# Reordering small pieces of work in the queues of a fused mLSTM and Fourier-mixing kernel

## Chip, core and metric

The kernel runs on one core of a Trainium2 chip. The metric is the device time of one execution in microseconds (us), the median of three runs. The profile is of one more execution; its span, 418.1 us from the first to the last instruction, is a little shorter than the time of that run, 419.82 us. TensorE is also called PE here, VectorE DVE, ScalarE ACT and GpSimd POOL, as the profile does.

## What is computed

The first half is an mLSTM cell over 4 batches, 8 heads, 768 steps and 40 features per head. The second half takes its output as 4 x 768 x 320, adds the real part of a two-dimensional Fourier transform, normalizes and applies a two-layer MLP with a residual.

```python
# mLSTM, for every step t
m_new = max(f[t] + m, i[t])
C = exp(f[t] + m - m_new) * C + exp(i[t] - m_new) * outer(v[t], k[t])
n = exp(f[t] + m - m_new) * n + exp(i[t] - m_new) * k[t]
y[t] = sigmoid(o[t]) * (C @ q[t]) / max(abs(n @ q[t]), 1)

# mixing, x is y as (4, 768, 320)
u  = x + real(fft(fft(x, axis=1), axis=2))
un = (u - mean(u)) / sqrt(var(u) + 1e-6)
out = u + relu(un @ w_ch1) @ w_ch2          # 320 -> 1280 -> 320
```

## The kernel before

The 768 steps of a batch are cut into six chunks of 128. Within a chunk the recurrence is two products: one from the state that the chunk before left (`from_state`), one from the chunk's own steps, weighed by an exponential and masked (`scores`, `weigh`, `from_chunk`). The result is copied out of PSUM (`gather`), transposed to have the steps on the partitions (`turn`) and divided by its denominator (`finish`). After that a batch is folded, transformed (`mix_seq`, `mix_feat`), added to x with its statistics (`mix_add`), centered, transposed and sent through the MLP. One batch's mLSTM runs beside the batch before's mixing and MLP.

Every engine works off its own instructions in the order in which the program has them. That order is a plan: `at(slot, phase, fn, ...)` puts a function at a slot, and within a slot at a phase. The phases of a slot are `EVAC` (0), `FILL` (1), `MAIN` (2) and `FILL_PE` (3); fractions are added to place a piece before or behind another. Slots are the steps of the MLP of some batch once it has begun (slot 31 for batch 0).

```python
    def mlstm_from_state(b, c):
        k = chunks[b, c]
        k.ph = ps_h.tile([L, NP, L], FP, name="ph", tag="ph")     # two banks serve ph, pc and late px
        if c > 0:
            ...                                                    # k.C x k.qg into k.ph

    def mlstm_to_state(b, c):
        k = chunks[b, c]
        if c < NT - 1:
            k.pc = ps_h.tile([L, NP, D1], FP, name="pc", tag="ph")
            ...                                                    # k.kn x k.vw into k.pc (+ the decayed state)

    def mlstm_gather(b, c):
        ...                                                        # k.pc -> C_next, k.ph -> k.hT
        if 0 < c < TG:                                             # first step of the chunk before
            nc.scalar.copy(out=hT_bufs[(b * NT + c - 1) % 2][:, :, 0:1], in_=k.ph[:, :, 0:1])
        nc.scalar.activation(out=k.so, in_=k.so, func=AF.Tanh, scale=0.5)

    def mlstm_turn(b, c, early):
        k = chunks[b, c]
        k.px = bank("px", [L, NP, L]) if early else ps_h.tile([L, NP, L], FP, name="px", tag="ph")
        for p in range(NP):
            nc.tensor.transpose(k.px[:, p, :], k.hT[:, p, :], ident)

    def plan_mlstm(b, s0, stride=3):
        for c in range(NT):
            s = s0 + stride * c
            ...
            at(s + 1, FILL, mlstm_mask, b, c)                      # b > 0, GpSimd
            at(s + 2, FILL, mlstm_weigh, b, c)                     # VectorE
            at(s + 3, FILL_PE, mlstm_from_state, b, c)
            at(s + 3, FILL_PE + 3, mlstm_from_chunk, b, c)
            at(s + 3, FILL_PE + 3, mlstm_to_state, b, c)
            at(s + 4, FILL, mlstm_gather, b, c)
            if b == 0:
                t, x = ((8, 11), (11, 14), (13, 14), (14, 15.5), (17, 18), (18, 21))[c]
            else:
                t = s + (8, 8, 7, 7 if b == 1 else 5, 5, 5)[c]
                x = t + 1
            at(t, FILL_PE + ((2.5 if c < 4 else 1) if b == 0 else 1), mlstm_turn, b, c, b == 0 and c < 4)
            at(x, FILL + 0.05, mlstm_finish, b, c)
```

The weights arrive as 64-bit floats and are made into 32-bit ones in ten pieces, each in three steps: `take` (VectorE extracts exponent and fraction from the words that a DMA brought), `convert` (ScalarE, two activations), `join` (VectorE, three operations).

```python
    def mlp_relu(b, gr, f):                                        # frees the bank pm
        nc.scalar.activation(out=hidden(gr, f), in_=mixes[b].pm[f % 2], func=AF.Relu, scale=-1.0)

    when += [((s, 0.7), (s + 1, 0.7), (s + 2, 0.6)) for s in (33, 36, 39, 42, 45)]
    ...
        for (s, phase), fn in zip(w, (p.take, p.convert, p.join)):
            at(s, FILL + phase, fn)
```

The addition to x (`mix_add`) frees the bank `pu` of the feature transform, which is then used for `pm` of the MLP. The reciprocal root of the variance is found by a bit trick on VectorE and three Newton steps of four operations on GpSimd; the MLP's output is scaled by it.

```python
    def mix_rstd(b):
        ...                                                        # VectorE: v = -(var + 1e-6) / 2, first y
        for _ in range(3):
            nc.gpsimd.tensor_tensor(out=t, in0=y, in1=y, op=OP.mult)
            nc.gpsimd.tensor_tensor(out=t, in0=t, in1=v, op=OP.mult)
            nc.gpsimd.tensor_scalar(out=t, in0=t, scalar1=1.5, scalar2=None, op0=OP.add)
            nc.gpsimd.tensor_tensor(out=y, in0=t, in1=y, op=OP.mult)
```

Of the kernel before, what the change touches and what calls it, by code (L numbers as in the profile page):

```python
# [10 lines left out]
FP = mybir.dt.float32  # L11
# [3 lines left out]
AF = mybir.ActivationFunctionType  # L15
OP = mybir.AluOpType
# [3 lines left out]
L = 128  # L20
NT = S // L
NP = H // 2
D1 = D + 1
# [3 lines left out]
NFF = DFF // L  # L27
# [23 lines left out]
def kernel(  # L51
# [14 lines left out]
    nc = tc.nc  # L66
# [13 lines left out]
    ps_h = pool("ps_h", 2, space=PSUM)  # L80
    ps_m = pool("ps_m", 1, space=PSUM)

    turn = iter("3210321032120312031230123012012301023130201320132013201320123021320321")
# [38 lines left out]
    def at(slot, phase, fn, *args):  # L122
        plan.setdefault((slot, phase), []).append((fn, args))
# [7 lines left out]
    EVAC, FILL, MAIN, FILL_PE = range(4)  # L131
# [249 lines left out]
    chunks = {}  # L381
# [91 lines left out]
    def mlstm_from_state(b, c):  # L473

        k = chunks[b, c]
        k.ph = ps_h.tile([L, NP, L], FP, name="ph", tag="ph")
        if c > 0:
            for p in range(NP):
                nc.tensor.matmul(k.ph[:, p, :], k.C[:, p, :], k.qg[:, p, :], start=(p == 0), stop=False,  # L479
                                 skip_group_check=True)  # L480
# [8 lines left out]
    def mlstm_to_state(b, c):  # L489
        k = chunks[b, c]  # L490
        if c < NT - 1:
            add = b == 0 and c > 0
            k.pc = ps_h.tile([L, NP, D1], FP, name="pc", tag="ph")
            for h in range(H):
                r0 = (h % 2) * 64
                nc.tensor.matmul(k.pc[r0:r0 + D, h // 2, :], k.kn[:, h, :], k.vw[:, h, :], start=(h < 2), stop=not add,
                                 skip_group_check=True)
            if add:
                for hip in range(2):
                    r = slice(hip * 64, hip * 64 + D)  # L500
                    nc.tensor.matmul(k.pc[r], ident[:, r], k.Cd, start=False, stop=True, skip_group_check=True)

    def mlstm_gather(b, c):
        k = chunks[b, c]
        k.hT = hT_bufs[(b * NT + c) % 2]
        if c < NT - 1:
            for hip in range(2):
                r, m = slice(hip * 64, hip * 64 + D), slice(hip * 64, hip * 64 + D1)
                Cv = k.C_next[r, :, m]
                if b == 0:  # L510
                    nc.scalar.copy(out=Cv, in_=k.pc[r])
                elif c == 0:
                    nc.vector.tensor_copy(out=Cv, in_=k.pc[r])
                else:
                    nc.vector.tensor_tensor(out=Cv, in0=Cv, in1=k.pc[r], op=OP.add)
        if c in BACKWARDS:
            nc.scalar.copy(out=k.hT[:, :, 1:], in_=backwards(k.ph, L - 1, L - 1))
            if c > TG:
                nc.scalar.copy(out=k.hT[:, :, 0:1], in_=k.ph[:, :, 0:1])
            else:  # L520
                nc.gpsimd.tensor_copy(out=k.hT[:, :, 0:1], in_=h_first)
        else:
            for r in (slice(0, L),) if c > 0 else (slice(hip * 64, hip * 64 + D1) for hip in range(2)):
                nc.scalar.copy(out=k.hT[r], in_=k.ph[r])  # L524
            if c == 0:
                nc.gpsimd.tensor_copy(out=h_first, in_=k.hT[:, :, 0:1])
        if 0 < c < TG:
            nc.scalar.copy(out=hT_bufs[(b * NT + c - 1) % 2][:, :, 0:1], in_=k.ph[:, :, 0:1])
        nc.scalar.activation(out=k.so, in_=k.so, func=AF.Tanh, scale=0.5)

    def mlstm_turn(b, c, early):
        k = chunks[b, c]
# [24 lines left out]
# [3 lines that stand above are left out]
            if b > 0:  # L560
                t = 22 + 2 * c if b == 1 and c < 3 else s - 5
                at(t, FILL, mlstm_load, b, c)
                at(t, FILL, mlstm_load_max, b, c)
                at(t, FILL, mlstm_load_decay, b, c)
                at(s, FILL, mlstm_load_o, b, c)
            if (b, c) > (0, 0):
                at(s, FILL, mlstm_exp, b, c, 0)
                at(s + 1, FILL - 0.5, mlstm_exp, b, c, NP)
                last = (b, c) == (0, NT - 1)
                at(s - 1 if last else s, FILL_PE + (2.05 if last else 2), mlstm_scores, b, c)  # L570
                if b > 0:
                    at(s + 1, FILL, mlstm_mask, b, c)
            at(s, FILL, mlstm_scale_v, b, c)
            at(s if (b, c) == (0, 2) else s + 1, FILL + 0.1, mlstm_scale_q, b, c)
            at(s + 2, FILL, mlstm_decay, b, c)
            end = (b, c) == (0, NT - 1)
            at(s + 1 if end else s + 2, FILL - 0.4 if end else FILL, mlstm_weigh, b, c)
            at(s + 2 if end else s + 3, MAIN - 0.1 if s + 3 in slots_of_halves else FILL_PE, mlstm_from_state, b, c)
            at(s + 2 if end else s + 3, FILL_PE + (2 if end else 3), mlstm_from_chunk, b, c)
            at(s + 3, FILL_PE + 3, mlstm_to_state, b, c)  # L580
            at(s + 3 if end else s + 4, FILL, mlstm_gather, b, c)
            if b == 0:
                t, x = ((8, 11), (11, 14), (13, 14), (14, 15.5), (17, 18), (18, 21))[c]
            else:
                t = s + (8, 8, 7, 7 if b == 1 else 5, 5, 5)[c]
                x = t + 1
            at(t, FILL_PE + ((2.5 if c < 4 else 1) if b == 0 else 1), mlstm_turn, b, c, b == 0 and c < 4)
            at(x, FILL + 0.05, mlstm_finish, b, c)


# [4 lines left out]
    mixes = {}  # L595
# [187 lines left out]
    def mix_rstd(b):  # L783

        k = mixes[b]
        v = st_p.tile([L, NT], FP, name="v", tag="v")
        y = k.rstd = st_p.tile([L, NT], FP, name="rstd", tag="rstd")
        t = st_p.tile([L, NT], FP, name="t", tag="t")
        nc.vector.tensor_scalar(out=v, in0=k.u[:, :, DM + 1], scalar1=1e-6, scalar2=None, op0=OP.add)
        nc.vector.tensor_scalar(out=t.bitcast(U32), in0=v.bitcast(U32), scalar1=1, scalar2=None,  # L790
                                op0=OP.logical_shift_right)
        nc.vector.tensor_scalar(out=y.bitcast(U32), in0=t.bitcast(U32), scalar1=-1.0, scalar2=float(0x5F3759DF),
                                op0=OP.mult, op1=OP.add)
        nc.vector.tensor_scalar(out=v, in0=v, scalar1=-0.5, scalar2=None, op0=OP.mult)
        for _ in range(3):
            nc.gpsimd.tensor_tensor(out=t, in0=y, in1=y, op=OP.mult)
            nc.gpsimd.tensor_tensor(out=t, in0=t, in1=v, op=OP.mult)
            nc.gpsimd.tensor_scalar(out=t, in0=t, scalar1=1.5, scalar2=None, op0=OP.add)
            nc.gpsimd.tensor_tensor(out=y, in0=t, in1=y, op=OP.mult)

    def plan_mix(b, s0, x_done, s_feat, s_add, s_turn):
        for j in range(TG):
# [298 lines left out]

    def plan_batch(b, s_mlstm, s_mix, s_mlp):
        plan_mlstm(b, s_mlstm)
        done = [s_mlstm + 3 * (j + NT // 2) + 7 + (b == 1 and j == 0) for j in range(NT // 2)]
        assert s_mix >= done[-1] and s_mlp >= s_mix + 9
        late = [s_mlp + 2 * c for c in range(TG)]
        if b == 0:
            feat = [s_mix + 1, s_mix + 1, s_mlp + 3]
            turn = [s_mix + 2, s_mix + 3, s_mix + 4]
            add = turn + [s_mlp, s_mlp + 4, s_mlp + 6]  # L1110
            late = [s_mlp + 2, s_mlp + 5, s_mlp + 7]
        else:
            feat = [s_mix + c for c in ((3, 4, 6) if b == 1 else (3, 4, 7))]
            add = [s_mix + c for c in ((4, 4, 5, 6, 7, 7) if b == 1 else (4, 4, 5, 6, 8, 9))]
            turn = [s_mix + c for c in ((5, 6, 6) if b == 1 else (6, 7, 8))]
            late = [s_mix + c for c in ((7, 8, 8) if b == 1 else (9, 10, 10))]
            at(s_mlp, EVAC + 0.5, mlp_sums)
        plan_mix(b, s_mix, done, feat, add, turn + late)
        at(s_mlp + NFF + (2 if b > 0 else 0), FILL + 0.6, mix_rstd, b)
        plan_mlp(b, s_mlp)  # L1120

    s_mlp = 31
# [9 lines left out]

    when = [((2, 0.7), (4, 0.5), (6, 0.6)), ((6, 0.7), (7, 0.5), (8, 0.6)), ((11, 0.7), (13, 0.5), (22, 0.6))]
    when += [((22, 0.7), (23, 0.7), (27, 0.6)), ((27, 0.7), (28, 0.7), (32, 0.6))]
    when += [((s, 0.7), (s + 1, 0.7), (s + 2, 0.6)) for s in (33, 36, 39, 42, 45)]
    pieces = w1_pieces + w2_pieces
    for n, (w, p) in enumerate(zip(when, pieces)):
        if n > 4:
# [125 lines left out]
```

## Time and profile before

| what | value |
|---|---|
| time, median of 3 | 420.55 us (419.62 to 420.63) |
| span in the profile | 418.1 us |
| PE matmul busy | 405.1 us, 2966 instructions |
| PE weight load busy | 304.0 us |
| VectorE busy | 287.8 us |
| ScalarE busy | 188.9 us |
| GpSimd busy | 115.3 us |
| granted TensorE clock | 1.0 |

How to read it: an engine's idle time only costs something if the engine that sets the end waits for it. The view of the waits of one engine lists who ended them, with the sum, the number and the longest. The timeline lists instructions in order of time: start, duration, engine, line of the kernel, operation, output and inputs, and in brackets the idle time of the engine just before and what ended it. An instruction that waits for several semaphores is put down to the one that the profile saw last, so a row has to be held against the ends of the instructions it may depend on. In the first third of the span (up to about 125 us) all engines have much to do: in the stretch from 100 to 110 us PE is busy for 10.00 us, VectorE for 9.63, GpSimd for 5.93 and ScalarE for 5.22.

### The profile page before, as it was taken

The numbers are of one execution on the slowest core, as the hardware profiler recorded it, in microseconds if no ns is written. First come the engines' busy times: TensorE is split into PE (matmuls) and PEld (weight loads), VectorE is DVE, ScalarE is ACT, GpSimd is POOL, SyncE is SP. The second block draws the span as 40 slices with busy tenths as digits, with TensorE's granted clock in tenths as the row PEclk, the third lists the DMA queues.
The fourth block names the chain that finished last, engine by engine and source line by source line (L and its number), as shares of the span: only waits on it lengthen the run. The fifth ranks groups of instructions, "written<-read, shape, count | busy, mean of one in ns | idle before, by whom it ended". The sixth has DMA issues, their size and how long they took to land.

```text
span 418.1 us, 8020 instructions
## 1 busy us (share of the span) xinstructions
PE 405.1 (97%) x2966; PEld 304.0 (73%) x2966; DVE 287.8 (69%) x682; ACT 188.9 (45%) x493; POOL 115.3 (28%) x194
## 2 busy tenths in 40 slices
PE   8999999999999999999999999989999999999997
PEld 6877454676667778767559998967559988555996
DVE  8789894767995638786874569786774686335652
ACT  6986375676661232655455413735442113355000
POOL 5564201459431520333061430333050000010000
PEclk9999999999999999999999999999999999999999
DMA  7889298467774154166200444210000000000010
GB/s 225 284 227 346 85 269 260 148 195 226 241 202 148 57 156 144 60 211 179 69 0 2 153 153 131 105 36 2 0 2 0 33 31 29 4 2 0 16 48 31
DMA packets 20549, 47.14 MB, mean 113 GB/s; under 512 B 2784, under 2 KB 9312, under 8 KB 20384
## 3 DMA queue, kind: packets, MB, share of 16 engines
q1 hardware_dynamic: 20512, 46.65, 36.5%
q8 instruction: 23, 0.38, 0.4%
q14 instruction: 14, 0.11, 0.1%
HBM read 42.52 MB, written 4.11 MB: 112 GB/s over the span
## 4 chain that ended last, share of the span: by engine, by line
PE 75%; DVE 14%; DMA 5%; ACT 2%; issue 2%; POOL 0%; DVEq 0%; ACTq 0%; POOLq 0%; SPq 0%
PE po L1031 18%; PE pm L912 16%; PE po L975 8%; PE pm L917 5%; PE ps L465 4%; PE ph L486 4%; DMA kvt<-in_kv 4%; PE ph L479 3%; PE pu L733 3%; PE pm L850 2%; DVE W L471 2%; PE px L535 2%; DMA qk<-in_qkT 2%; PE pz L702 2%; PE put L776 1%
## 5 line engine op out<-in xcount | busy, mean ns | idle before, releaser
L981 DVE SCALAR_TENSOR_TENSOR x<-po,rstd,x 128x160 f32<-128x160 f32 (+1 forms) x69 | 26.9, 394 | 41.2 <-PE po L1031 35.5
L921 DVE TENSOR_TENSOR h<-h,pm 128x384 f32<-128x384 f32 x60 | 30.6, 549 | 32.5 <-PE pm L917 19.4
L421 ACT ACTIVATE W<-W,colT 128x128 f32<-128x128 f32 x144 | 45.0, 396 | 0.0
L443 POOL TENSOR_SCALAR_AFFINE_SELECT W<-W 128x1024 f32<-128x1024 f32 x18 | 21.9, 1218 | 80.6 <-ACT W L421 56.3
L912 PE MATMUL pm<-uT,w_sb 128*128 128x384 f32 x90 | 37.5, 503 | 0.2 <-DVE uT L900 0.2
L975 PE MATMUL po<-w_sb,h 128*128 128x320 f32 x120 | 34.4, 435 | 0.0
L471 DVE TENSOR_TENSOR W<-ps,W 128x512 f32<-128x512 f32 x48 | 30.7, 680 | 4.5 <-POOL W L443 4.3
L850 PE MATMUL pm<-uT,w_sb 128*128 128x384 f32 x80 | 30.0, 500 | 1.6 <-DMA qk<-in_qkT 0.9
L781 ACT COPY uT<-put 128x384 f32<-128x384 f32 x24 | 11.2, 478 | 39.8 <-PE put L776 39.8
L975 PEld LDWEIGHTS po<-w_sb,h 128*128 128x128 f32 x120 | 22.2, 190 | 9.5 <-issue 0.8
L1031 PE MATMUL po<-T,S 128*128 128x160 f32 x180 | 27.9, 302 | 0.3 <-DVE x L981 0.3
L465 PE MATMUL ps<-qk 40*128 40x128 f32 x384 | 27.4, 282 | 0.0
L465 PEld LDWEIGHTS ps<-qk 40*128 40x128 f32 x384 | 23.7, 187 | 4.7 <-issue 0.7
L1031 PEld LDWEIGHTS po<-T,S 128*128 128x128 f32 x180 | 25.5, 190 | 1.7 <-DVE x L981 0.5
L1031 PE MATMUL po<-w_sb,h 128*128 128x160 f32 x180 | 26.4, 301 | 0.0
L1031 PEld LDWEIGHTS po<-w_sb,h 128*128 128x128 f32 x180 | 25.1, 190 | 1.3 <-DVE x L981 0.3
L431 POOL TENSOR_TENSOR qg<-qk,Gb 128x512 f32<-128x512 f32 x18 | 25.7, 1430 | 0.9 <-DMA Gb<-G_d 0.8
L486 PE MATMUL ph<-W,kvt 128*41 128x128 f32 x384 | 25.8, 277 | 0.0
L524 ACT COPY h<-ph 41x512 f32<-41x512 f32 (+1 forms) x16 | 9.3, 583 | 36.2 <-PE ph L486 36.1
L912 PEld LDWEIGHTS pm<-uT,w_sb 128*128 128x128 f32 x90 | 15.5, 189 | 13.7 <-DVE h L921 6.0
L479 PEld LDWEIGHTS ph<-qg,C 128*128 128x128 f32 x160 | 20.0, 191 | 6.3 <-issue 2.6
L479 PE MATMUL ph<-qg,C 128*128 128x128 f32 x160 | 21.6, 278 | 2.9 <-DVE x L550 1.8
(207 smaller groups left out, 845.6 us busy)
## 6 DMA issues: line engine op xcount, KB each, us to landing
W<-M_d SPq DMA_DIRECT2D x18, 512.0 KB
kvt<-in_kv SPq DMA_DIRECT2D x24, 324.0 KB
qk<-in_qkT SPq DMA_DIRECT2D x48, 160.0 KB
raw<-in_w SPq DMA_DIRECT2D x10, 640.0 KB
Gb<-G_d SPq DMA_DIRECT2D x36, 128.0 KB
so<-in_o SPq DMA_DIRECT2D x24, 160.0 KB
out<-x SPq DMA_DIRECT2D x24, 160.0 KB
ds_sb<-in_dft_s SPq DMA_DIRECT2D x1, 1155.0 KB
```

The lines of the kernel that those rows point to most:

```text
L421: nc.scalar.activation(out=k.W[:, h, :], in_=M, func=AF.Exp, scale=-1.0, bias=colT[:, c, 0, b * H + h:b * H + h + 1])
L431: nc.gpsimd.tensor_tensor(out=k.qg, in0=k.qk[:, 0], in1=k.Gb, op=OP.mult)
L465: nc.tensor.matmul(k.ps[hip][:, p, :], k.qk[r, 1, p, :], k.qk[r, 0, p, :], start=True, stop=True)
L471: nc.vector.tensor_tensor(out=Wv, in0=k.ps[hip], in1=Wv, op=OP.mult)
L479: nc.tensor.matmul(k.ph[:, p, :], k.C[:, p, :], k.qg[:, p, :], start=(p == 0), stop=False, skip_group_check=True)
L486: nc.tensor.matmul(k.ph[hip * 64:hip * 64 + D1, p, :], k.v1[:, 2 * p + hip, :], k.W[:, 2 * p + hip, :], start=(c == 0 and p == 0), stop=Tr ...
L850: nc.tensor.matmul(k.pm[i], w1_sb[:, ch, f0:f0 + L], u[2 * ch], start=(ch == 0 and not ahead), stop=(ch == 1 and ahead), skip_group_check= ...
L912: nc.tensor.matmul(bank, w, u, start=start, stop=True, skip_group_check=True)
L921: nc.vector.tensor_tensor(out=h, in0=h, in1=bank, op=OP.add)
L975: nc.tensor.matmul(k.po, hidden(gr, f)[:, i * L:(i + 1) * L], w2_sb[:, f, :], start=(f == 0), stop=(f == NFF - 1))
L981: nc.vector.scalar_tensor_tensor(out=u, in0=po, scalar=k.rstd[:, c:c + 1], in1=u, op0=OP.mult, op1=OP.add)
L1031: nc.tensor.matmul(po, a[:, f], w[:, f], start=start and f == 0, stop=f == half - 1, skip_group_check=True)
```

## The change

Nothing is computed differently. Six things are moved:

- In batch 0, chunk 4, the tile `pc` is taken from the pool ahead of `ph`, so that the two exchange their banks; and the transposes of chunks 0 and 1 stand a slot later, behind the product from the state of the chunk after.
- The conversion and the join of the sixth weight piece are a slot later, so that the conversion, which waits for a DMA by way of VectorE, doesn't stand ahead of relus.
- In batches 1 to 3 the tanh of the output gate stands behind the centering of the same slot.
- The last of batch 0's six additions is a slot earlier.
- Batch 0's first guess of the reciprocal root is two slots later, and its Newton steps are spread three slots apart.
- In batches 2 and 3 the transposes of the fourth chunk, and so its `finish` and the first `fold`, are two slots (the fold one slot) later.

```diff
     def mlstm_from_state(b, c):
         k = chunks[b, c]
+        if (b, c) == (0, NT - 2):
+            k.pc = ps_h.tile([L, NP, D1], FP, name="pc", tag="ph")
         k.ph = ps_h.tile([L, NP, L], FP, name="ph", tag="ph")
...
-            k.pc = ps_h.tile([L, NP, D1], FP, name="pc", tag="ph")
+            if not hasattr(k, "pc"):
+                k.pc = ps_h.tile([L, NP, D1], FP, name="pc", tag="ph")
...
-        nc.scalar.activation(out=k.so, in_=k.so, func=AF.Tanh, scale=0.5)
+        if b == 0:
+            mlstm_tanh(b, c)
+
+    def mlstm_tanh(b, c):
+        so = chunks[b, c].so
+        nc.scalar.activation(out=so, in_=so, func=AF.Tanh, scale=0.5)
...
+            if b > 0:
+                at(s + 4, FILL + 0.35, mlstm_tanh, b, c)
             if b == 0:
-                t, x = ((8, 11), (11, 14), (13, 14), (14, 15.5), (17, 18), (18, 21))[c]
+                t, x = ((9, 11), (12, 14), (13, 14), (14, 15.5), (17, 18), (18, 21))[c]
             else:
-                t = s + (8, 8, 7, 7 if b == 1 else 5, 5, 5)[c]
+                t = s + (8, 8, 7, 7, 5, 5)[c]
                 x = t + 1
-            at(t, FILL_PE + ((2.5 if c < 4 else 1) if b == 0 else 1), mlstm_turn, b, c, b == 0 and c < 4)
+            at(t, FILL_PE + ((1.95 if c < 2 else 2.5 if c < 4 else 1) if b == 0 else 1), mlstm_turn, ...)
...
-        for _ in range(3):
-            ...                                  # the four GpSimd operations
+        k.newton = v, t
+
+    def mix_rstd_step(b):
+        ...                                      # the same four, once
...
-        done = [s_mlstm + 3 * (j + NT // 2) + 7 + (b == 1 and j == 0) for j in range(NT // 2)]
+        done = [s_mlstm + 3 * (j + NT // 2) + 7 + (b > 0 and j == 0) for j in range(NT // 2)]
...
-            add = turn + [s_mlp, s_mlp + 4, s_mlp + 6]
+            add = turn + [s_mlp, s_mlp + 4, s_mlp + 5]
...
-        at(s_mlp + NFF + (2 if b > 0 else 0), FILL + 0.6, mix_rstd, b)
+        s = s_mlp + NFF + 2
+        at(s, FILL + 0.6, mix_rstd, b)
+        for n in range(3):
+            at(s + 3 * n if b == 0 else s, FILL + 0.65, mix_rstd_step, b)
...
-    when += [((s, 0.7), (s + 1, 0.7), (s + 2, 0.6)) for s in (33, 36, 39, 42, 45)]
+    when += [((33, 0.7), (35, 0.7), (36, 0.6))] + [((s, 0.7), (s + 1, 0.7), (s + 2, 0.6)) for s in (36, 39, 42, 45)]
```

More of the change, by code (lines that the diff above doesn't have):

```diff
@@ L581, in plan_mlstm @@
             at(s + 3 if end else s + 4, FILL, mlstm_gather, b, c)
+            if b > 0:
+                at(s + 4, FILL + 0.35, mlstm_tanh, b, c)
             if b == 0:
-                t, x = ((8, 11), (11, 14), (13, 14), (14, 15.5), (17, 18), (18, 21))[c]
+                t, x = ((9, 11), (12, 14), (13, 14), (14, 15.5), (17, 18), (18, 21))[c]
             else:
-                t = s + (8, 8, 7, 7 if b == 1 else 5, 5, 5)[c]
+                t = s + (8, 8, 7, 7, 5, 5)[c]
                 x = t + 1
-            at(t, FILL_PE + ((2.5 if c < 4 else 1) if b == 0 else 1), mlstm_turn, b, c, b == 0 and c < 4)
+            at(t, FILL_PE + ((1.95 if c < 2 else 2.5 if c < 4 else 1) if b == 0 else 1), mlstm_turn, b, c, b == 0 and c < 4)
             at(x, FILL + 0.05, mlstm_finish, b, c)
@@ L794, in mix_rstd @@
         nc.vector.tensor_scalar(out=v, in0=v, scalar1=-0.5, scalar2=None, op0=OP.mult)
-        for _ in range(3):
[L796 to L799, printed above, removed]
+        k.newton = v, t
+    def mix_rstd_step(b):
+        k = mixes[b]
+        y, (v, t) = k.rstd, k.newton
+        nc.gpsimd.tensor_tensor(out=t, in0=y, in1=y, op=OP.mult)
+        nc.gpsimd.tensor_tensor(out=t, in0=t, in1=v, op=OP.mult)
+        nc.gpsimd.tensor_scalar(out=t, in0=t, scalar1=1.5, scalar2=None, op0=OP.add)
+        nc.gpsimd.tensor_tensor(out=y, in0=t, in1=y, op=OP.mult)
     def plan_mix(b, s0, x_done, s_feat, s_add, s_turn):
```

## The prediction

> **What bounds the kernel now.** I read the page's busy line first, then the waits of TensorE, then the timelines of all engines around each wait.
>
> ```profile
> PE 405.1 (97%) x2966; PEld 304.0 (73%) x2966; DVE 287.8 (69%) x682; ACT 188.9 (45%) x493; POOL 115.3 (28%) x194
> ```
>
> TensorE (PE) is busy 405.1 of 418.1 us. The change adds or removes no matmul, so it can only win back idle time: 418.1 - 405.1 = 13.0 us. Of that, 1.25 us lie before the first matmul and about 3 us after the last one (413.51 + 1.52 = 415.0): some 8.7 us are left. The waits of PE say where (total, times, longest, in us):
>
> ```profile
> PE ph L479 <- DVE x L550: 1.8, 3, 1.3
> ...
> PE put L776 <- ACT uc L769: 1.2, 4, 0.4
> PE pm L850 <- DMA qk<-in_qkT: 0.9, 1, 0.9
> PE ph L479 <- POOL eo L622: 0.8, 1, 0.8
> PE px L535 <- ACT h L519: 0.8, 1, 0.8
> PE px L535 <- ACT h L528: 0.8, 2, 0.4
> PE pm L850 <- DVE x L753: 0.5, 1, 0.5
> ```
>
> These seven rows sum to 6.8 us, and the parts of the change aim at most of them. So 420.55 - 8.7 = 411.9 us is the floor if every gap closed, just at the 2% mark (412.1).
>
> The second stage to read is that of slots 33 to 37, in the timeline of all engines from 66 to 78 us (start, duration, engine, line; in brackets the idle time before):
>
> ```profile
> 68.64 0.49 DVE L344 TENSOR_SCALAR e<-raw 128x640 uint32<-128x640 uint32 x1 [6.17 <-DMA raw<-in_w]
> ...
> 69.17 0.83 ACT L351 ACTIVATE e<-e,ebias 128x640 uint32<-128x640 uint32 x1 [3.94 <-DVE e L344]
> ...
> 69.91 0.72 ACT L352 ACTIVATE m<-m 128x640 f32<-128x640 uint32 x1
> 70.53 0.85 ACT L865 ACTIVATE h<-pm 128x384 f32<-128x384 f32 x2
> ...
> 71.05 0.91 PE L850 MATMUL pm<-uT,w_sb 128*128 128x384 f32 x2 [0.90 <-DMA qk<-in_qkT]
> ```
>
> A weight piece lands at 68.6, VectorE (DVE) takes it, ScalarE (ACT) converts it, and only then comes the relu that empties the bank for the next pm matmul. That relu's input was complete at about 66.2 (last L841). The matmul starts at 71.05, right after the first relu's end (70.53 + 0.48 = 71.0): the wait is the relu's, not the DMA's that the row names.
>
> The third is batch 3's fifth chunk:
>
> ```profile
> 278.32 0.49 DVE L550 TENSOR_TENSOR x<-px,so 128x320 f32<-128x320 f32 x1
> 278.96 1.13 PE L479 MATMUL ph<-qg,C 128*128 128x128 f32 x8 [1.26 <-DVE x L550]
> ```
>
> PE's ph needs the bank from which VectorE has just finished the third chunk; the two px groups before it (275.37 and 277.10) took both banks of that pool.
>
> **What the Trainium skill says.** "PSUM — Partial Sum Buffer", section "Engine vs sequencer instructions": the queues of ScalarE, VectorE and GpSimd are strict FIFO, and matmuls start and complete in program order. The trace agrees: the relu sat behind a conversion that was itself waiting, with ScalarE idle for 3.94 us. "Perfetto Trace Analysis", section "Tensor Engine Instruction": the profiler estimates a matmul's end, so I reckon from starts: four transposes are listed at 0.66 us, but the next group starts 0.49 us after them (23.44 to 23.93). "SBUF — State Buffer", section "SBUF: two separate sides": GpSimd and a VectorE operation with two SBUF inputs take turns on one port pair for whole instructions. The trace fits: Newton's first operations on 128x6 take 0.78, 0.66 and 0.81 us beside VectorE, later ones 0.20.
>
> **The change part by part.**
>
> *First batch (0 to 54 us).* Transposes of chunks 0 and 1 now stand behind the next chunk's ph. At 23.44 and 29.06 px waited 0.41 and 0.40 for the last small copy (L528 ends at 23.38); ph needs only the state copies (22.71). So ph starts at about 22.93 (end of the pM group), px follows at 23.8 with its input ready. Gain up to the second transpose: 0.41 + 0.40 = 0.8, with restart about 0.9. It doesn't all survive. VectorE runs without a real gap from 24.5 to 41 us and does not move, so px of chunk 3 must wait for chunk 1's finish (bank read until 34.60 + 0.49 = 35.09); it started at 35.78, so 0.65 is left. The rest of the chain then shifts with it: state copies, ph of chunk 5 (39.74 to about 39.05), its output, copy, last px (43.12 to 42.4). VectorE's weighing of chunk 5 ends at 39.95, still ahead of its use (40.55). The pc/ph exchange of chunk 4 swaps two banks: ph of chunk 5 starts at 39.74 while ph of chunk 4 is still being copied (39.66 to 40.25), so it already stands in pc's bank; I give the swap nothing. **0.7 us.**
>
> *Conversion and addition (66 to 78 us).* The conversion moves one slot later, behind the relus: the 0.90 gap goes (0.97 by starts). The scores behind it then wait until VectorE has weighed both ps banks (70.73), some 0.4 us of that back. Then put waits 0.28 for uc, which sat behind so's tanh (0.37 by starts) and ScalarE's late queue; the earlier relu and the tanh behind it free it. Then pm waits 0.52 for the addition L753 that frees the bank of pu (76.77 to 77.26); the addition now stands a slot earlier, ahead of the join (2.4 us) and the next piece's extraction (0.9 us), at about 72 to 73 us. Starts: 0.97 + 0.35 + 0.59 = 1.9, and the scores' 0.4 falls inside time that put then no longer waits. **1.85 us.**
>
> *Newton's steps (92 to 118 us).* Twelve GpSimd operations stood between 91.92 and 97.27, ahead of the mask:
>
> ```profile
> 97.35 1.09 POOL L443 TENSOR_SCALAR_AFFINE_SELECT W<-W 128x1024 f32<-128x1024 f32 x1
> 98.41 1.28 POOL L431 TENSOR_TENSOR qg<-qk,Gb 128x512 f32<-128x512 f32 x1
> ```
>
> The mask's other inputs are there by about 94.3 (the copies of h), so mask, weighing and qg come 3 us earlier, and VectorE, full from 98.5 to 118, starts its backlog earlier. PE waited 0.30 (99.74, for qg) and 0.17 (117.26, for a finish). Three steps of four operations, three slots apart, cost about 0.9 us each and fit: rstd is first used ten slots after the first. **0.45 us.**
>
> *Fourth chunks' transposes of batches 2 and 3 (two slots later).* ph of chunk 5 then finds a bank that was free long ago. The waits of 0.38 (184.34) and 1.26 (278.96) go; by starts 0.55 and 1.43. Against it: finish (1.7 us) and fold (1.7 us) of this chunk now stand in VectorE's queue behind the weighing and ahead of the next finish and the addition L921. In batch 3: state copy until 284.0, weighing to 285.3, finish 287.0, fold 288.7, next finish 290.4, L921 290.95, which the tails L917 want at about 290.85 (292.25 now, less 1.43). So 0.15 to 0.2 us may come back in each. **0.35 + 1.25 us.**
>
> *Tanh behind the centering (batches 1 to 3).* At 265.03 put waited 0.42 for uc, which ran at 264.37 behind a tanh that started at 264.00: **0.37 us**. Nothing else waits for a tanh; it is used slots later.
>
> Sum: 0.7 + 1.85 + 0.45 + 1.6 + 0.37 = 5.0 us. These are gaps I can name; the ones that open behind them I can't, and VectorE and the DMAs stand close behind PE in the first third. I take a fifth off: **4.0 us**, 420.55 - 4.0 = 416.55, say **416.5 us**.
>
> **The rivals.** (1) *A transfer takes the place.* From 50 to 70 us the DMA engines are full (0.9 to 1.07 busy in every 2 us), and the piece at 68.6 comes at the end of that queue. Weighing of batch 1's first chunk stands behind it on VectorE, so PE earlier by 0.7 buys nothing there. For: 6.17 us of VectorE idle. Against: the queue starts when VectorE is through with an older piece (49.74), which moves a little too. It would cost the 0.7 and part of the 1.85: 417.5 to 418. (2) *VectorE becomes the bound* in 98 to 125 and 284 to 291 us: it is 7.6 to 9.6 of 10 busy there. If the tails of batches 2 and 3 wait a full finish (1.7 us) each, the fourth-chunk part is worth nothing: 418.5. (3) *All of it passes through*, because the gaps are real PE idle and later stages (120 to 250 us) show almost none: 415.5.
>
> **Range and chances.** Rival 3 gives the low end, rivals 1 and 2 together the high one: **414.9 to 419.0**. A run varies by 0.5 us either way (419.62 to 420.63). Over 2% faster would need all 8.7 us: 0.01. Slower by 2% would need new waits of 8 us, more than any queue here moved: 0.01. Within 2%: 0.98.
>
> **What would show it.** PE's waits: the rows for L528, for the DMA at pm L850, for L753 and the 1.3 at L550 gone, those for POOL eo L622 and L519 about as before or smaller. Relu L865 directly behind its matmuls, ahead of L351. The mask at 94 to 95 us instead of 97.35, less the shift. Starts against before: pm after the third put (57.67) 0.7 earlier; pm at 77.40 some 2.5 earlier; batch 1's last ph chunk at 117 about 3 earlier; the last L1031 group 4 to 5 earlier. Wrong if the shift at 77 is under 1.5, if ph at 279 waits elsewhere, or if L917 waits over 0.5 us for L921 in batches 2 and 3.

## The result, and the profile after

The changed kernel took 416.41 us (median of 4 runs, 416.04 to 417.03) against 420.59 us for the kernel before (median of 4): a ratio of 0.9907, with a 95% interval from 0.9888 to 0.9926. The profiled span went from 418.1 to 414.8 us. The prediction was 416.5 us, so the total was met; the steps under it were not all met, and the rest of this text is about them.

The page's busy line of the changed kernel:

```profile
PE 404.3 (97%) x2966; PEld 304.4 (73%) x2966; DVE 289.8 (70%) x682; ACT 189.2 (46%) x493; POOL 117.1 (28%) x194
```

And the view of its PE's waits (engine, line, what was waited for: us in total, times, longest):

```profile
...
PE px L544 <- DVE den L553: 1.1, 1, 1.1
PE ph L482 <- POOL qg L431: 1.0, 1, 1.0
PE ph L482 <- POOL eo L633: 0.8, 1, 0.8
PE px L544 <- ACT h L523: 0.8, 1, 0.8
PE put L787 <- ACT uc L780: 0.5, 2, 0.3
...
PE ph L482 <- DVE x L559: 0.2, 1, 0.2
```

No work was added or removed, and the busy line is nearly the same; VectorE and GpSimd are busy for 2.0 and 1.8 us more, with the same number of instructions. The rows that went are those of the prediction: the two waits for the small copy (0.8 together), the DMA named at the MLP's pm (0.9), the addition at pm (0.5), and of the 1.8 for the finish x only 0.2 is left, the wait at 117 us. But the first two rows are new. They are the places where gains were handed back.

**Where the time went.** I matched each matmul of the changed kernel with the same one of the kernel before and followed the difference of their starts. The changed profile began its first `ps` matmul at 7.72 us instead of 7.22, ahead of anything that was changed; that half microsecond belongs to the start and is taken off. A plus is a gain:

| stretch of the kernel before | gained | lost again | net | predicted |
|---|---|---|---|---|
| 23 to 37 us, first batch | 1.13 | 1.31 | -0.18 | 0.7 |
| 66 to 80 us, conversion and addition | 2.27 | 1.29 | 0.98 | 1.85 |
| 92 to 100 us, Newton | 0.57 | 0 | 0.57 | 0.45 |
| 184 us, fourth chunk of batch 2 | 1.06 | 0.44 | 0.62 | 0.35 |
| 265 us, tanh | 0.35 | 0 | 0.35 | 0.37 |
| 279 us, fourth chunk of batch 3 | 1.93 | 0.44 | 1.50 | 1.25 |
| sum | | | 3.84 | 5.0, less a fifth: 4.0 |

The 0.44 in the fourth chunks is no loss: it is the four transposes that have left one place and now stand two slots later. Of the first row nothing is left and of the second about half; the others are as predicted or a little fuller. Outside the rows another 0.09 is lost at 268 to 270 us, so the last product starts 3.76 earlier.

In the changed kernel's timeline (start, us, engine, line, operation, in brackets the idle time before), the relu is now ahead of the conversion. The piece landed (start of the row in L344) at 68.58 instead of 68.64 us, which is 0.56 earlier against the start of the pass:

```profile
66.91 0.87 ACT L880 ACTIVATE h<-pm 128x384 f32<-128x384 f32 x2 [1.01 <-PE pm L856]
...
68.58 0.49 DVE L344 TENSOR_SCALAR e<-raw 128x640 uint32<-128x640 uint32 x1 [5.44 <-DMA raw<-in_w]
...
69.11 0.83 ACT L351 ACTIVATE e<-e,ebias 128x640 uint32<-128x640 uint32 x1 [0.18 <-DVE e L344]
...
69.27 2.20 PE L865 MATMUL pm<-uT,w_sb 128*128 128x384 f32 x6
```

PE's six matmuls run through without the gap of 0.90, and ScalarE stands idle for 0.18 us ahead of the conversion instead of 3.94. Ten microseconds later, in the same timeline, PE waits for another chain:

```profile
74.85 0.66 POOL L530 COPY h_first<-h 128x4 f32<-128x4 f32 x1 [8.89 <-ACT h L528]
...
75.47 1.68 POOL L443 TENSOR_SCALAR_AFFINE_SELECT W<-W 128x1024 f32<-128x1024 f32 x1
...
77.12 1.82 POOL L431 TENSOR_TENSOR qg<-qk,Gb 128x512 f32<-128x512 f32 x1
...
79.00 1.16 PE L482 MATMUL ph<-qg,C 128*128 128x128 f32 x8 [1.02 <-POOL qg L431]
```

GpSimd has three operations in a row, without a gap, and the last, q times the gate, ends where PE starts. Its queue was idle for 8.89 us before, since the copy `h_first` stands at its head and waits for ScalarE. The three operations also take longer than in the kernel before, whose timeline shows them at the same place:

```profile
75.34 0.33 POOL L526 COPY h_first<-h 128x4 f32<-128x4 f32 x1 [10.05 <-ACT h L524]
...
75.63 1.35 POOL L443 TENSOR_SCALAR_AFFINE_SELECT W<-W 128x1024 f32<-128x1024 f32 x1
...
76.95 1.28 POOL L431 TENSOR_TENSOR qg<-qk,Gb 128x512 f32<-128x512 f32 x1
```

From the start of `h_first` to the end of qg they took 2.88 us before and 4.10 now. What stands beside them on VectorE is now the join, which moved together with the conversion, and its last operation is stretched in turn (0.82 us before). VectorE's timeline of the changed kernel:

```profile
74.64 0.83 DVE L358 SCALAR_TENSOR_TENSOR e<-raw,e 128x640 uint32<-128x640 uint32 x1
...
75.38 0.82 DVE L360 SCALAR_TENSOR_TENSOR m<-raw,m 128x640 f32<-128x640 uint32 x1
...
76.23 1.59 DVE L364 TENSOR_TENSOR w_sb<-m,e 128x640 f32<-128x640 f32 x1
```

The Newton steps are where the prediction wanted them, behind the mask, which moved from 97.35 to 92.18. GpSimd's timeline of the changed kernel:

```profile
92.18 1.27 POOL L443 TENSOR_SCALAR_AFFINE_SELECT W<-W 128x1024 f32<-128x1024 f32 x1 [0.37 <-DMA Gb<-G_d]
...
98.23 0.20 POOL L811 TENSOR_TENSOR t<-rstd 128x6 f32<-128x6 f32 x1 [1.63 <-DVE v L805]
```

### The profile page after: what moved, and what is told of

Read it like the earlier page. It is cut to its first block, busy times and chain, and to the rows that moved or that the text cites. A ratio compares the mean times of both kernels' runs of the same rounds, so it can differ in the third digit from the quotient of the medians.

```text
span 414.8 us, 8020 instructions
## 1 busy us (share of the span) xinstructions
PE 404.3 (97%) x2966; PEld 304.4 (73%) x2966; DVE 289.8 (70%) x682; ACT 189.2 (46%) x493; POOL 117.1 (28%) x194
## 4 chain that ended last, share of the span: by engine, by line
PE 83%; DVE 9%; DMA 2%; ACT 2%; POOL 1%; issue 1%; SPq 0%; ACTq 0%; POOLq 0%; DVEq 0%
PE po L1046 18%; PE pm L927 17%; PE po L990 8%; PE pm L932 6%; PE pm L865 5%; PE ph L489 5%; PE ps L465 4%; PE ph L482 4%; PE pu L744 3%; PE px L544 2%; PE pm L856 2%; PE pz L713 2%; PE put L787 2%; PE pz L701 1%; DMA qk<-in_qkT 1%; DVE W L471 1%
## 5 line engine op out<-in xcount | busy, mean ns | idle before, releaser
L983 ACT ACTIVATE h<-h 128x384 f32<-128x384 f32 x45 | 23.1, 521 | 2.0 <-DVE h L936 2.0
```

## The experiments

Twelve kernels were run. The first four each put one part of the change into the kernel before; they were timed together against 420.07 us of that kernel. The next four change one thing in the changed kernel, against 419.79 us of the kernel before; the last four again, against 420.25 us, with the changed kernel itself among them.

**The first batch alone** (the bank exchange and the transposes of chunks 0 and 1).

```diff
+        if (b, c) == (0, NT - 2):
+            k.pc = ps_h.tile([L, NP, D1], FP, name="pc", tag="ph")
-                t, x = ((8, 11), (11, 14), (13, 14), ...
+                t, x = ((9, 11), (12, 14), (13, 14), ...
+            ... 1.95 if c < 2 else 2.5 if c < 4 ...
```

> The kernel before with the first-batch part alone (bank exchange of chunk 4, transposes of chunks 0 and 1 behind the next ph). If the prediction's step holds, 0.7 us less than before (about 419.9). If the wait only moves to the transposes of chunk 3, which read a bank that VectorE frees late, as the trace of the whole change suggests (they waited 1.14 us there), 0 us within 0.3, or slightly more than before.

Measured: 420.06 us, ratio 1.0001 [0.9985, 1.0016]. The two waits for the small copy are gone from PE's waits, and in their place stands the wait for the finish of chunk 1, as in the changed kernel. From this run's timeline of PE:

```profile
37.66 0.63 PE L538 MATMUL px<-ident,h 128*128 128x128 f32 x4 [1.14 <-DVE den L547]
```

So this wait comes with this part and needs no other. The part alone is worth nothing that these runs can measure.

**Conversion and addition alone.**

```diff
+    when += [((33, 0.7), (35, 0.7), (36, 0.6))] + [... for s in (36, 39, 42, 45)]
-            add = turn + [s_mlp, s_mlp + 4, s_mlp + 6]
+            add = turn + [s_mlp, s_mlp + 4, s_mlp + 5]
```

> The kernel before with the sixth piece's conversion and join and the sixth addition moved, nothing else. The prediction's step: 1.85 us less, some of it (0.37) needing the tanh's move too, so 1.5 to 1.85 less (about 418.9). The rival from the trace: the next ph then waits for qg on GpSimd for about 1 us, and 0.6 to 1.0 us are left (about 419.8).

Measured: 419.79 us, ratio 0.999 [0.998, 1.0]: 0.3 us, at most 0.8, where 1.85 were predicted. The rows for the DMA and for the addition at pm are gone, and q times the gate has become a row of 1.0 in two waits, the longer of which is this one in PE's timeline (GpSimd's three operations take 4.10 us here too):

```profile
79.16 1.05 PE L479 MATMUL ph<-qg,C 128*128 128x128 f32 x7 [0.68 <-POOL qg L431]
```

By starts this profile gained 0.98 us up to 80 us against the one of the kernel before, as much as the whole change did. The next run shows why the times may say less.

**Newton's steps alone.**

```diff
-        at(s_mlp + NFF + (2 if b > 0 else 0), FILL + 0.6, mix_rstd, b)
+        at(s_mlp + NFF + 2, FILL + 0.6, mix_rstd, b)
+        for n in range(3):
+            at(s + 3 * n if b == 0 else s, FILL + 0.65, mix_rstd_step, b)
```

> The kernel before with Newton's steps spread and batch 0's first guess two slots later. The prediction's step: 0.45 us less. Rival: GpSimd's queue was not what PE waited for, 0.0 us.

Measured: 419.19 us, ratio 0.9977 [0.9962, 0.9991]: 0.9 us. The starts show two gains. From 87 to 112 us the difference goes from -1.33 to -1.90, so 0.57, the same as in the whole change. But it was at -1.33 by then, and -0.31 (the start of the pass) up to 63 us. The 1.02 between them lie where the conversion stands, which this kernel doesn't move. Its timeline there:

```profile
67.31 0.49 DVE L344 TENSOR_SCALAR e<-raw 128x640 uint32<-128x640 uint32 x1 [5.15 <-DMA raw<-in_w]
67.84 0.83 ACT L351 ACTIVATE e<-e,ebias 128x640 uint32<-128x640 uint32 x1 [2.92 <-DVE e L344]
```

The piece landed at 67.31 instead of 68.64 us, the relu behind the conversion ran at 69.20 instead of 70.53, and PE's waits have no row for the DMA at pm. The kernel above with the first batch's part and the next one have no such row either, with the conversion in its old place. Two of these three kernels have the same instructions as the kernel before up to there. So the wait of 0.90 us that the prediction priced need not be there in every execution: it was in the one profile of the kernel before, and how often it comes is not known.

**The fourth chunks alone.**

```diff
-                t = s + (8, 8, 7, 7 if b == 1 else 5, 5, 5)[c]
+                t = s + (8, 8, 7, 7, 5, 5)[c]
-        done = [... + 7 + (b == 1 and j == 0) ...]
+        done = [... + 7 + (b > 0 and j == 0) ...]
```

> The kernel before with the transposes of the fourth chunks of batches 2 and 3 two slots later. The prediction's step: 1.6 us less (0.35 and 1.25), with 0.15 to 0.2 us given back at the tails in each. Rival: the tails wait for a whole finish on VectorE, 0.3 us less or none.

Measured: 417.38 us, ratio 0.9942 [0.9925, 0.9959]: 2.7 us. By starts, the two stretches gave 0.62 and 1.50, the same as in the whole change, so 2.1 in sum against 1.6 predicted. This profile also has the piece's earlier landing at 68 us (0.97 gained) and a longer wait for a finish at 117 us (0.28 lost); whether the times' surplus of 0.6 comes from there is not shown.

**q times the gate of batch 1, chunk 1 a slot earlier**, in the changed kernel.

```diff
-            at(s if (b, c) == (0, 2) else s + 1, FILL + 0.1, mlstm_scale_q, b, c)
+            at(s if (b, c) in ((0, 2), (1, 1)) else s + 1, FILL + 0.1, mlstm_scale_q, b, c)
```

> The changed kernel with batch 1, chunk 1's qg one slot earlier in GpSimd's queue, ahead of the mask that waits for ScalarE. If the wait of 1.02 us of ph at 79 us is GpSimd's chain h_first, mask, qg (7.1 us idle before it), about 1.0 us less than the changed kernel (415.4). If ph waits for something else just as long (its state copy, its bank), 0 us.

Measured: 415.59 us, ratio 0.9906 [0.9876, 0.9937]. The row for qg is gone and ph starts at once (PE's timeline of this run):

```profile
78.03 1.05 PE L482 MATMUL ph<-qg,C 128*128 128x128 f32 x8
```

That is 0.97 us earlier than in the changed kernel though this profile began 0.20 later. So the wait of 1.02 was GpSimd's queue, and the conversion's gain was handed back to it. The gain is not kept whole: the `ps` products behind it take 1.51 us instead of 1.06, since they need the banks that VectorE is still weighing (79.43 to 80.72), and from 82 us on the kernel is 0.62 earlier (0.8 against its own start).

**The transposes of chunk 3 behind the product of chunk 4**, in the changed kernel, so that they don't wait for the finish of chunk 1.

```diff
-                ... (13, 14), (14, 15.5), (17, 18), ...
+                ... (13, 14), (15, 15.5), (17, 18), ...
-            ... 1.95 if c < 2 else ...
+            ... 1.95 if c in (0, 1, 3) else ...
```

> The changed kernel with chunk 3's transposes of batch 0 behind chunk 4's ph, a slot later. If the first batch's gain was lost because these transposes wait 1.14 us for VectorE to read chunk 1 out of their bank, 0.7 to 1.1 us less than the changed kernel (about 415.5). If VectorE's queue itself sets the pace (weighing of chunk 5 ends at 40.7 us), under 0.3 us.

Measured: 417.16 us, ratio 0.993 [0.9911, 0.9949]. The row is gone. Against the start of the pass ph of chunk 4 starts 1.67 us earlier than in the changed kernel (1.2 without the four transposes that left their place ahead of it), but the mixing's first product only 0.9 and the last instruction only 0.4. PE's waits have a new row of 0.3 for VectorE's fold, which is part of the 0.5 that is lost in the mixing. (The wait of 0.8 ahead of ph of chunk 5 is as long as before, with another name, the state copy.) Going around VectorE in one place meets it in the next. The two edits together (`both`) say the same:

> Both of these moves on the changed kernel. If the two are independent, the sum of their gains, 1.7 to 2.1 us, about 414.5. If a transfer binds between (the weight piece that lands at 68.6 us), the first batch's gain is lost there and only qg's 1.0 us remains.

Measured: 415.64 us, ratio 0.9898 [0.9877, 0.9918]; by its time no more than the earlier q times the gate alone, by starts 0.4 more.

**Without the exchange of the banks**, in the changed kernel (the three lines about `pc` taken out of `mlstm_from_state`).

> The changed kernel without the exchange of the banks of pc and ph in chunk 4, all else kept. The prediction gives the exchange nothing: the time of the changed kernel within 0.2 us. Rival: the exchange saves ph of chunk 4 or 5 a wait for copies of the chunk before (up to 0.6 us more without it).

Measured: 416.78 us, ratio 0.9918 [0.9895, 0.9941]. The exchange is worth nothing that can be measured, as predicted. The wait for the finish of chunk 1 was 0.5 us here instead of 1.1; the next run shows that it can be 0.5 with the exchange too. By starts this profile ends 0.6 ahead of the changed kernel's first one, which is that shorter wait.

**The changed kernel once more.**

> The changed kernel once more, untouched, on the chip that runs the next three kernels, as their yardstick: 416.4 us as before, between 415.8 and 417.1. Its first 20 us may differ from the other profile of the same kernel, since the first matmuls start at a changing pace; all later rows should stand alike once this is taken off.

Measured: 416.79 us (416.26 to 418.99), ratio 0.9934 [0.9912, 0.9956]. The same program, with the wait at 0.5 us too. Here are two executions of it in the timeline, first that of the result above, with GpSimd's qg, VectorE's finish of chunk 1 and PE's px:

```profile
34.19 1.28 POOL L431 TENSOR_TENSOR qg<-qk,Gb 128x512 f32<-128x512 f32 x1
...
34.69 1.13 DVE L557 SCALAR_TENSOR_TENSOR so<-so,den 128x320 f32<-128x320 f32 x1
...
36.48 0.63 PE L544 MATMUL px<-ident,h 128*128 128x128 f32 x4 [1.14 <-DVE den L553]
```

And the same place in the timeline of the second execution:

```profile
34.75 0.49 DVE L557 SCALAR_TENSOR_TENSOR so<-so,den 128x320 f32<-128x320 f32 x1
...
35.48 1.27 POOL L431 TENSOR_TENSOR qg<-qk,Gb 128x512 f32<-128x512 f32 x1 [1.30 <-DMA so<-in_o]
...
35.92 0.63 PE L544 MATMUL px<-ident,h 128*128 128x128 f32 x4 [0.50 <-DVE den L553]
```

In the first, qg began half a microsecond ahead of the operation on `so`, and this took 1.13 us; in the second, qg waited for a DMA, came 1.3 us later, and the operation took 0.49. In both executions it takes 0.49 wherever GpSimd is idle, in 15 cases out of 15. The finish of the first chunk, 4.6 us ahead, is stretched to 1.50 us in both: qg runs from 30.00 to 31.27 and the operation on `so` begins at 30.11. In the kernel before it began at 29.62, ahead of qg (29.86), and took 0.63, and qg was the one that got longer (1.52 instead of 1.27). "SBUF — State Buffer", section "SBUF: two separate sides", of the Trainium skill says that the two engines take turns on a port for whole instructions, and these rows agree. So the wait ahead of chunk 3 is made of a VectorE that is late anyway and of this stretch, which differs between executions of one program: the stretch is 0.64 us longer in the first, and so is the wait. Both profiles without the exchange have the short form (0.49), but of the seven with it and with all of VectorE's work only this one; so the exchange isn't needed for the stretch to stay away, and whether it makes the stretch likelier is open.

**Less work for VectorE.** To see whether VectorE's queue is what chunk 3 waits for, the second weight piece's join leaves out two of its three operations (sign and sum of the halves; that piece of the weights is then not fully converted), some 1.6 us at 25 to 27 us.

```diff
+            if self is not w1_pieces[1]:
                 nc.vector.scalar_tensor_tensor(out=self.e, in0=self.hi, ...)
                 nc.vector.scalar_tensor_tensor(out=m, in0=self.lo, ...)
```

> The changed kernel without the two VectorE operations that join the second weight piece (some 1.6 us of VectorE's work at 25 to 27 us); part of that piece's conversion is left out. If VectorE's queue is what the first batch waits for after the exchange (theory: the finish of chunk 1 and the fold come late because VectorE is late), the wait of 1.14 us ahead of the transposes of chunk 3 shrinks below 0.4 and everything from 37 to 70 us lies 0.6 to 1.1 us earlier against the start of the pass; the time is 0.3 to 1.0 us below the changed kernel's. If the exchange of the banks itself is to blame (rival: the px bank comes free late whatever VectorE does before), the wait stays at 1.1 and the time within 0.2.

Measured: 415.94 us, ratio 0.9898 [0.988, 0.9917], 0.85 below the changed kernel beside it. The row is gone, in PE's timeline of this run px starts right behind the `ps` products:

```profile
34.79 0.66 PE L545 MATMUL px<-ident,h 128*128 128x128 f32 x4
```

Against the changed kernel's first profile the starts up to 34 us are 0.35 earlier, and all from 37 us to the end about 1.65: 1.3 us, the wait and a little more, and none of it is lost up to the last instruction. That decides for VectorE's queue and against the exchange of the banks as what this wait is for. The operation on `so` was stretched less here (0.91 and 0.66 us for the first two chunks), so the run shortens the queue in two ways at once. Two of its four times lie below all of the changed kernel's.

**The tanh back in its old place.**

> The changed kernel with the tanh back at the end of the gather for all batches. By the prediction 0.37 us more than the changed kernel (from the 0.35 that the trace shows between 190 and 265 us); the rival is nothing, if the wait for ScalarE's uc ahead of the MLP's input of batches 2 and 3 is no longer than it now is, 0.3 each.

Measured: 416.04 us, ratio 0.9908 [0.9889, 0.9927], 0.75 below the changed kernel beside it, whose runs it overlaps. The times don't show the 0.37. The starts do: at 256 us this kernel is 0.16 ahead of the changed one's first profile, at 268 us 0.11 behind it, so 0.27 were lost at the place named. PE's wait for uc ahead of put, 0.5 in two waits with the change, is 1.3 in four without. One of those that come back is at 75 us, where the wait for qg swallows it (it falls from 1.0 to 0.7); so only the one at 263 us shows in the end.

**The best of it: earlier qg, no exchange.**

> The changed kernel with q times the gate of batch 1, chunk 1 a slot earlier (0.8 less by the earlier run) and without the exchange of the banks of pc and ph in the first batch's fourth chunk. If both gains are real and add up: 0.9 to 1.6 us less than the changed kernel, 414.8 to 415.5. If the weight piece's landing at some 68.6 us takes up what the first batch gains before it: no more than 0.8 less, 415.6, as with the q times gate alone.

Measured: 415.01 us (414.07 to 417.70), ratio 0.9891 [0.9865, 0.9917]: the fastest median of all, 1.8 below the changed kernel beside it, but with runs that overlap. I would not credit the edit with 1.8: the profile began 0.94 us earlier than that of the changed kernel and ended 1.15 earlier, so it accounts for 0.2, after the piece's landing and VectorE's weighing took their part again. It is faster than the kernel before (415.01 against 420.25); whether it is faster than the changed kernel is not shown.

## Why the prediction came out, step by step

**First batch, 0.7: wrong.** The two waits went as described (1.13 gained, 0.9 predicted). The failed step is "VectorE ... does not move, so px of chunk 3 must wait for chunk 1's finish (bank read until 35.09)". I took that finish as it stood, and it came later: the bank was read until 36.34 (35.85 + 0.49), and px waited 1.14 us. Less the 0.49 by which this profile runs later from its start, that is 0.76 later than before. The second overlap with a qg makes 0.60 of it (the operation on `so` took 0.53 us before and 1.13 now). The first makes only 0.16: `so` took 0.87 us longer (0.63, now 1.50), but in the kernel before the same qg had stretched another operation, the `take` of a weight piece, from 0.48 us (as in the changed kernel) to 1.04. From VectorE's timeline of the kernel before:

```profile
29.62 0.63 DVE L548 SCALAR_TENSOR_TENSOR so<-so,den 128x320 f32<-128x320 f32 x1
...
30.69 1.04 DVE L344 TENSOR_SCALAR e<-raw 128x640 uint32<-128x640 uint32 x1
```

The prediction had named the port that the two engines share, and used it for Newton's operations alone. An engine without gaps that "does not move" moves back when its own operations grow. In the second execution, where the second overlap fell away, the first batch gained 0.43 us. `vector_less` shows that px waits for VectorE's queue; that the stretch makes it late is shown by the two executions, for the second overlap.

**Conversion and addition, 1.85: half of it.** The gaps that were named closed, 2.27 by starts. Two things failed. The sum left out what stands behind: q times the gate on GpSimd, which PE met with a wait of 1.02 us; `qg_early` took it away and got most of it back. The chain ahead of it was late because its operations had grown: with its old 2.88 us it would have ended at 77.7, before PE was ready at 77.98 (an estimate from the rows above). It took 4.10 to 4.15 us in all seven profiles with the moved join and qg behind the mask, and 2.88 in the four with the join in its old place. No run moved the join alone, so that the join does it is argued from the rows. And 0.97 of the sum was a wait from one profile that three other kernels with the conversion in its old place didn't have; their piece landed about a microsecond earlier against the pass. That may be why the part alone is worth only 0.3 us in time. Rival 1, that the transfer takes the place, was not what happened: PE waited for no transfer there in the changed kernel. (The DMA engines were at 0.9 to 1.07 from 52 to 68 us only; the prediction's first and last two microseconds, 50 to 52 and 68 to 70, have 0.54 and 0.88.)

**Newton, 0.45: right in the sum,** 0.57 by starts, in both kernels that have it. But it all came at the first of the two waits that were named, for qg at 99.74. The second, 0.17 for a finish at 117.26, is still there with the same length (the last of PE's rows above): that finish came earlier by no more than PE did. The part alone measured 0.9 us in time; its profile gained more than that, and the surplus there is the landing.

**Fourth chunks, 1.6: too small,** 2.1 by starts in both kernels that have it. The term that was mis-sized is the 0.15 to 0.2 us each that "may come back" when the tails of the MLP wait for the addition behind the finish. PE's timeline of the changed kernel in batch 3, at ph of chunk 5:

```profile
275.33 1.05 PE L482 MATMUL ph<-qg,C 128*128 128x128 f32 x8
```

And the addition and the tail, from the timelines of VectorE and PE:

```profile
288.32 0.54 DVE L936 TENSOR_TENSOR h<-h,pm 128x384 f32<-128x384 f32 x1
...
288.99 1.56 PE L932 MATMUL pm<-uT,w1t_sb 64*128 64x384 f32 x8
```

ph of chunk 5 has no wait ahead of it, and the addition ends at 288.86, 0.13 us before the tail begins; in batch 2 the margin is the same (196.00 and 196.13). So VectorE, the bound of rival 2, had 0.13 us to spare, and nothing came back.

**Tanh, 0.37: 0.35 by starts, and 0.27 when it is taken out.** Too small for the times to show.

**The bank exchange, nothing: right,** as far as 0.5 us can be told.

**The total.** By starts 3.84, by times 4.2, predicted 4.0. The steps that were too high (first batch by 0.9, conversion by 0.9) and those too low (0.1 and 0.5) leave 1.2 too much, and the fifth that I took off "for the gaps that open behind them" was 1.0. The deduction had the right reason, since both losses are gaps that opened behind; its size was luck. The single parts' times add up to 0.0 + 0.3 + 0.9 + 2.7 = 3.9, each with 0.4 to 0.7 us of doubt.

**The signs.** Of the rows that were to go all went, and relu and mask stand where they were expected. The starts say less for the account. Each against the start of its own pass, the pm behind the third put is 0.18 later (0.7 earlier predicted), the pm at 77.40 is 2.03 earlier (2.5), but from 80 us on only 0.81 is kept, the last ph of batch 1 is 1.38 earlier (about 3), and the last group 3.76 (4 to 5).

What stays open: the changed kernel's second profile gained 0.43 us in the first batch, where the first lost 0.18, and lost 0.52 again at 116 us, where ph waited 0.69 for a finish on VectorE (0.17 in the first); `vector_less` was not held up there. Why VectorE was later in the one than in the other was not tried.

## What to carry to other kernels

A gap closed in a stage where three engines are full is worth what the next engine in line leaves of it: ask for each closed gap which operation PE reaches next, when its inputs are ready now, and take the lesser. Then look at what the moved operations come to stand beside: here both losses lay where VectorE and GpSimd ran at once and one stretched the other. The gaps behind which nothing else came late (the fourth chunks, here at 184 and 279 us) kept all of the gain and carried more than half of the total. And a wait that ends on a transfer should be looked up in a second execution before it is priced: here it was 0.9 us in one and nothing in three others.

## What I had not expected of the hardware

- The same VectorE operation (`so`, 128x320 with two SBUF inputs) took 0.49 us alone and up to 1.50 us when it began just behind GpSimd's qg. Without the second such overlap, in another execution of the same program, a wait of 1.14 us was 0.50. In the kernel before there were overlaps too, but on operations that stood elsewhere in the queue.
- The first `ps` matmul began between 6.90 and 9.55 us in the fourteen profiles, with no edit ahead of it. In the latest one, the eight `pM` matmuls of L218 are listed at 1.92 and 1.80 us instead of 1.15 and 1.05. The times carry this spread of the start, and differences of half a microsecond are better read from the starts.
